# Reordering the build-time lists of stages, attention visits and PE transposes in a four-layer attention kernel

## The chip, the cores and the metric

One core of a Trainium2 chip; the experiments ran on three chips, each time with the kernel before in the same rounds. Time is device time of one execution in microseconds (us), the median of several executions. All executions told of here ran in the fast state; the mean clock granted to TensorE is 0.98 to 0.99 in every profile except one experiment, which is marked. Engines: PE is TensorE's matmul stream, PEld its weight loads, DVE is VectorE, ACT is ScalarE, POOL is GpSimd, SP is SyncE. "Attention run 1" and "attention run 2" are the two stretches with 1024 exponentials each (layers 1 and 3); the prediction calls them run 1 and run 2.

## The reference, cut to what matters

Four layers over x[2048, 1024], each with LayerNorm ahead and a residual after. Layers 0 and 2 (A) are linear attention with softmax feature maps, layers 1 and 3 (B) ordinary softmax attention; 32 heads of 32.

```python
def _A_ref(x, wqkv, w_phi, wo):          # linear attention
    # ... q, k, v: [1, 32, 2048, 32]
    pq = einsum("bhsd,hdf->bhsf", q, w_phi); pk = einsum("bhsd,hdf->bhsf", k, w_phi)
    phi_q = concat([softmax(pq), softmax(-pq)]); phi_k = concat([softmax(pk), softmax(-pk)])
    kv  = einsum("bhsf,bhsd->bhfd", phi_k, v);  z = phi_k.sum(s)
    o   = einsum("bhqf,bhfd->bhqd", phi_q, kv) / (einsum("bhqf,bhf->bhq", phi_q, z) + 1e-6)
    return o.reshape(B, S, D) @ wo
def _B_ref(x, wqkv, wo):                 # softmax attention
    p = softmax(einsum("bhqd,bhkd->bhqk", q, k) * 32 ** -0.5)
    return einsum("bhqk,bhkd->bhqd", p, v).reshape(B, S, D) @ wo

x = A_x
x = x + _A_ref(_layernorm(x), A_wqkv, A_w_phi, A_wo)
x = x + _B_ref(_layernorm(x), B_wqkv, B_wo)
x = x + _A_ref(_layernorm(x), A_wqkv, A_w_phi, A_wo)
x = x + _B_ref(_layernorm(x), B_wqkv, B_wo)
```

(Formulas shortened; the einsum that sums z over s is written out.)

## The kernel before

The file is a list scheduler. A clock model with generators runs while the program is built; `pick` takes the first ready task of a window, attention steps go ahead of tasks, and what comes out is one fixed order of instructions per engine. Three tables are its input:

- `STAGES`: the order of tasks. `AK` and `PQ`/`PS` are key and query work of an A layer by chunks of 512 rows, `DN` its denominators and numerators, `AO` its output tiles, `fold` a folding of weights; `('BP', layer, chunk, quarters)` is Q, K and V of a B layer, with eight head groups in four quarters; `('BO', layer, t0, t1)` its output tiles.
- `VIS1`, `VIS3`: attention visits of layers 1 and 3: first query tile, width in tiles, key chunks, whether it continues a partial sum, whether it is the last, and the head groups.
- `TR`: the chunks whose 128x128 transposes run on PE; all others go through a transposing DMA.

```python
def x_chain(l, t, key):                  # residual tile t behind layer l
    yield ("key", key)
    xb = yield from grab(t_x)
    yield dma(xb[:], xsrc(l, t), 256)
    # ... add, LayerNorm, store

def emit_step():                         # one attention step: score matmuls, then two exponentials
    u = units[st["ui"]]
    # ...
        for e in range(2):
            for j in range(2):
                # ...
                nc.tensor.matmul(ring_t[bufs[e]][:, j, i * n:(i + 1) * n], lhsT=K2[e][c]...,
                                 rhs=u.Q[r, e, 0:n], start=True, stop=True, ...)
    for e in range(2):
        clk.start(exp_chain(u, kks, e, bufs[e]), st["t"] + PE_LAT)

# in the main loop:
        if ready and len(ring.free) >= 2:
            emit_step()                  # attention first
            continue
        start_burst()
        if cur_u[0] is not None:
            emit_sum()                   # E.V and E.ones of earlier steps
            continue
        if cur[0] is None:
            cur[0] = pick()              # then a task of STAGES
        # ...
                if sum(x[1] for x in recent) < WARM * HAM:
                    set_mode("col")      # filler: nobody reads the result
                    for j in range(4):
                        nc.tensor.matmul(work[-1][32 * j:32 * (j + 1), :], lhsT=ones[:], rhs=idb, ...)

# in the Q projection's post, for the first two visits of layers 1 and 3 (three tokens in t_here):
                here = vi is not None and bool(t_here.free) and not t_here.wait
                if here:
                    # ... hand the Q tile to attention directly
                yield dma(qd[l, c, g][:], b2, 256)   # otherwise attention loads it back from DRAM
```

In a task's matmul group "full width" means one 128x128 matmul of 512 columns; while attention is active the group is issued as four narrow ones of 32 output rows each. A "score matmul" multiplies queries with keys; its result is what an exponential of attention reads.

The softmax here doesn't subtract the row's maximum and nothing guards it: scores larger than these inputs give would overflow.

## Time and profile before

| | before |
|---|---|
| median (3 executions) | 2384.27 us (2383.03 to 2387.67) |
| span of the profiled execution | 2380.4 us |
| front, until the first exponential of layer 1 | 289.4 us |
| attention run 1; of it ACT idle | 1003.0 us; 20.8 us |
| middle, between the two runs | 126.7 us |
| attention run 2; of it ACT idle | 953.1 us; 4.7 us |
| tail | 8.2 us |

In an attention run ACT is all but full; in front and middle PE and the waits of PE decide. The prediction shows the lines of the page.

### The profile page before, as it was taken

The numbers are of one execution on the slowest core, as the hardware profiler recorded it, in microseconds if no ns is written. First come the engines' busy times: TensorE is split into PE (matmuls) and PEld (weight loads), VectorE is DVE, ScalarE is ACT, GpSimd is POOL, SyncE is SP. The second block draws the span as 40 slices with busy tenths as digits, with TensorE's granted clock in tenths as the row PEclk, the third lists the DMA queues.
The fourth block names the chain that finished last, engine by engine and source line by source line (L and its number), as shares of the span: only waits on it lengthen the run. The fifth ranks groups of instructions, "written<-read, shape, count | busy, mean of one in ns | idle before, by whom it ended". The sixth has DMA issues, their size and how long they took to land.

```text
span 2380.4 us, 81956 instructions
## 1 busy us (share of the span) xinstructions
PE 2245.8 (94%) x35942; PEld 1009.7 (42%) x35985; DVE 1321.7 (56%) x2398; ACT 2121.0 (89%) x2501; POOL 400.5 (17%) x502
## 2 busy tenths in 40 slices
PE   6898999999999999998999899999999999999998
PEld 3544544334434333434555453433333333333555
DVE  6885554454545468696567855554533274363223
ACT  5543499999999999999998459999999999999998
POOL 3311101110211112122212210020200031120111
PEclk9999999899999999999999999999999999999999
DMA  6453364364454345354234655554465432230001
GB/s 249 145 157 108 132 193 171 112 199 130 147 141 145 108 133 155 115 142 80 91 101 130 173 135 166 192 140 137 123 198 174 135 125 81 64 110 33 19 22 31
DMA packets 216343, 306.05 MB, mean 129 GB/s; under 512 B 98736, under 2 KB 112560, under 8 KB 213296
## 3 DMA queue, kind: packets, MB, share of 16 engines
q1 hardware_dynamic: 191792, 200.14, 28.9%
q0 software_dynamic: 24192, 100.67, 12.6%
q8 instruction: 281, 4.60, 0.8%
q14 instruction: 78, 0.64, 0.1%
HBM read 195.36 MB, written 86.51 MB: 118 GB/s over the span
## 4 chain that ended last, share of the span: by engine, by line
PE 70%; ACT 16%; issue 7%; DVE 6%; DMA 1%; POOL 0%; SPq 0%; ACTq 0%; DVEq 0%; POOLq 0%
PE work L460 25%; PE work L1524 15%; ACT E L1449 14%; PE ring L1469 14%; PE work L463 7%; PE work L1642 3%; PE ring L463 3%; DVE blk L446 2%; ACT blk L772 1%; DVE sm L814 1%; PE work L1038 1%; DMA xnT<-blk 1%; DMA slab<-in_A_wqkv_dram 0%; DVE kvacc L446 0%; PE work L848 0%
## 5 line engine op out<-in xcount | busy, mean ns | idle before, releaser
L1449 ACT ACTIVATE E<-ring 128x1024 bf16<-128x1024 f32 x2048 | 1901.7, 1211 | 26.6 <-PE ring L1469 23.2
L1524 PE MATMUL work<-E,V 128*32 128x512 bf16 (+2 forms) x5888 | 551.1, 319 | 9.6 <-issue 3.7
L1524 PE MATMUL work<-E,ones 128*32 128x512 bf16 (+2 forms) x5888 | 551.0, 319 | 4.0 <-issue 4.0
L1469 PE MATMUL ring<-Q,K2b 32*128 32x512 bf16 (+2 forms) x2896 | 394.0, 315 | 49.4 <-ACT E L1449 38.1
L446 DVE TENSOR_TENSOR blk<-blk,work 128x512 f32<-128x512 f32 (+1 forms) x301 | 203.7, 680 | 375.5 <-PE work L1524 321.9
L1469 PE MATMUL ring<-Q,K2a 32*128 32x512 bf16 (+2 forms) x2896 | 407.8, 318 | 1.6 <-DMA Q<-qd 0.6
L1524 PEld LDWEIGHTS <-V 128*32 128x32 bf16 x5888 | 243.9, 97 | 158.0 <-issue 70.2
L446 POOL TENSOR_TENSOR blk<-blk,blk 64x512 bf16<-64x512 f32 (+2 forms) x180 | 175.1, 973 | 777.3 <-DVE blk L1314 689.4
L1278 DVE COPY blk<-work 128x512 f32<-128x512 f32 (+2 forms) x184 | 97.1, 528 | 346.4 <-PE work L1524 341.4
L1469 PEld LDWEIGHTS <-K2a 32*128 32x128 bf16 x2944 | 119.3, 91 | 385.1 <-issue 372.9
L1524 PEld LDWEIGHTS <-ones 128*32 128x32 bf16 x5888 | 239.5, 97 | 51.8 <-issue 5.9
L1314 DVE RECIPROCAL blk<-blk 128x128 f32<-128x128 f32 x254 | 229.4, 930 | 2.6
L1642 PE MATMUL work<-ident,ones 128*32 128x512 bf16 x3156 | 222.0, 382 | 2.8 <-DVE blk L446 0.9
L1469 PEld LDWEIGHTS <-K2b 32*128 32x128 bf16 x2944 | 163.3, 91 | 135.5 <-issue 128.7
L460 PE MATMUL work<-slab,blk 128*32 128x512 bf16 x2752 | 179.9, 381 | 0.5 <-DVE blk L1278 0.2
L460 PE MATMUL work<-slab,xnT 128*32 128x512 bf16 (+1 forms) x2560 | 156.5, 367 | 0.9 <-DVE kvacc L446 0.3
L460 PE MATMUL work<-xnT,slab 128*32 128x512 bf16 x2120 | 140.5, 384 | 4.2 <-DMA xnT<-blk 2.5
L463 PEld LDWEIGHTS <-xnT 128*128 128x128 bf16 x818 | 79.1, 99 | 89.9 <-issue 17.2
L460 PEld LDWEIGHTS <-blk 128*32 128x32 bf16 x3404 | 78.4, 96 | 90.5 <-issue 32.9
L463 PE MATMUL work<-slab,xnT 128*128 128x512 bf16 (+1 forms) x485 | 106.7, 373 | 5.5 <-DMA slab<-in_A_wqkv_dram 3.0
L1642 PEld LDWEIGHTS <-ones 128*32 128x32 bf16 x3156 | 71.2, 95 | 89.8 <-issue 40.7
L460 PEld LDWEIGHTS <-slab 128*32 128x32 bf16 x3016 | 70.8, 96 | 86.1 <-issue 35.8
(184 smaller groups left out, 2321.8 us busy)
## 6 DMA issues: line engine op xcount, KB each, us to landing
pd<-blk SPq DMA_DIRECT2D x154, 256.0 KB, 2.5
blk<-pd SPq DMA_DIRECT2D x154, 256.0 KB, 3.4
Q<-qd SPq DMA_DIRECT2D x121, 256.0 KB, 2.8
slab<-in_B_wqkv_dram POOLq DMA_DIRECT2D x30, 1024.0 KB, 6.6
qd<-blk SPq DMA_DIRECT2D x64, 256.0 KB, 2.8
x<-blk SPq DMA_DIRECT2D x48, 256.0 KB, 2.7
blk<-x SPq DMA_DIRECT2D x48, 256.0 KB, 3.8
blk<-in_A_x_dram SPq DMA_DIRECT2D x32, 256.0 KB, 3.9
```

Of the source, the lines that this page charges most:

```text
L446: return ("op", e, cost, lambda x: eng(x).tensor_tensor(out=o, in0=a, in1=b, op=op))
L460: nc.tensor.matmul(o[js], lhsT=l[:, js], rhs=r, start=st, stop=sp, tile_position=(0, 32 * j), skip_group_check=True)
L463: nc.tensor.matmul(o, lhsT=l, rhs=r, start=st, stop=sp, skip_group_check=True)
L772: yield ("op", "S", c_act(C), lambda x, s=s: nc.scalar.activation(out=e[:, s * C:(s + 1) * C], in_=src, func=ACT.Exp, scale=1.0 - 2.0 * s))
L814: yield ("op", "V", c_sb(1024), lambda x: nc.vector.reduce_sum(out=sm[:, 0:32], in_=e3, axis=AX.X))
L1038: nc.tensor.matmul(bank[:, o:o + P], lhsT=e[:, s * C + t * P:s * C + (t + 1) * P], rhs=kvm[:, (2 * gp + gi) * 2 + s, :], start=True, stop= ...
L1278: yield ("op", "V", c_ps(n), lambda e: nc.vector.tensor_copy(out=a, in_=bank[:, 0:n]))
L1314: yield ("op", "V", 0.06 + 0.0063 * P, lambda e, x=x: nc.vector.reciprocal(out=r[:, x:x + P], in_=r[:, x:x + P]))
L1449: yield ("op", "S", c_act(2 * n), lambda x: nc.scalar.activation(out=E[:, :, 0:n], in_=ring_t[buf][:, :, 0:n], func=ACT.Exp, scale=INV_SQR ...
L1469: nc.tensor.matmul(ring_t[bufs[e]][:, j, i * n:(i + 1) * n], lhsT=K2[e][c][u.g // 4][r, u.g % 4, m, :], rhs=u.Q[r, e, 0:n], start=True, st ...
L1524: nc.tensor.matmul(u.acc[r0 + 32 * j:r0 + 32 * j + 32, 0:n], lhsT=lh, rhs=E[:, j, i * n:(i + 1) * n], start=u.first, stop=end, tile_positi ...
L1642: nc.tensor.matmul(work[-1][32 * j:32 * (j + 1), :], lhsT=ones[:], rhs=idb, start=True, stop=True, tile_position=(0, 32 * j), skip_group_c ...
```

## The change

Its intent, in its own words: output tiles wait for all residual tiles of the preceding stage; a slab (1 MB of weights) that a ready task lacks is loaded at once; stages and visits come in another order. The tables are long; here the code parts whole and of the tables what the argument uses.

```diff
 def x_chain(l, t, key):
     yield ("key", key)
+    if l % 2:
+        for i in range(NT):
+            yield ("key", ("xo", l - 1, i))
     xb = yield from grab(t_x)
...
+def slab_rank(s):            # slab_next, plus PEN where the task still needs something
...
+def slab_force():            # load the slab of a ready task into a free slot
...
-        want = sorted((slab_next(s), s) for s in slab_use)
+        want = sorted((slab_rank(s), s) for s in slab_use)
...
+        if left and slab_force():          # only where the scheduler would report "stuck"
+            continue
         if left:
             ...
             raise RuntimeError(f"stuck at ...
+PEN = 0
...
 VIS1 = (      # 28 visits, now 36, the first four:
-    (0, 4, (0,), False, False, (4, 5)), (0, 4, (0,), False, False, (0, 1, 3)), (0, 4, (0,), False, False, (2,)),
-    (0, 4, (0,), False, False, (6, 7)), ...
+    (0, 4, (0,), False, False, (4, 5)), (0, 4, (0,), False, False, (0, 1, 3)),
+    (0, 4, (0,), False, False, (6, 7)), (0, 4, (0,), False, False, (2,)), ...
 VIS3 = (      # the first visits:
-    (0, 4, (0,), False, False, (4, 5)), (0, 4, (0,), False, False, (0, 1, 2, 3)),
-    (0, 4, (0,), False, False, (6, 7)), (0, 4, (1,), True, False, (0, 1, 2, 3)), ...
+    (0, 4, (0,), False, False, (0, 1, 2, 3, 4, 5, 6, 7)), (0, 4, (1,), True, False, (0, 1, 2, 3)), ...
 STAGES = (    # all reordered; the start, and the start of layer 3:
-    ('AK', 0, 0, (0,), (0,)), ('AK', 0, 1, (0,), (0,)), ('fold', ('pk', 0)), ('fold', ('pk', 1)), ...
-    ('DN', 2, 1), ('BP', 3, 0, (1,)), ('BP', 3, 0, (0,)), ('AO', 2, 2), ('BP', 3, 0, (2, 3)), ('AO', 2, 1), ...
+    ('AK', 0, 0, (0,), (0,)), ('AK', 0, 0, (0,), (1,)), ('AK', 0, 1, (1,), (0,)), ('fold', ('pk', 0)), ...
+    ('BP', 3, 0, (1,)), ('DN', 2, 1), ('BP', 3, 0, (0,)), ('BP', 3, 0, (2,)), ('AO', 2, 1), ('BP', 3, 0, (3,)), ...
-TR = {(0, 'D', 0), (0, 'D', 2), (0, 'D', 3), (0, 'K', 0), (0, 'K', 1), (0, 'O', 0), (0, 'O', 1), (0, 'O', 2), (1, 'B', 0), (2, 'D', 0), (2, 'D', 3)}
+TR = {(0, 'D', 0), (0, 'D', 1), (0, 'D', 3), (0, 'K', 0), (0, 'K', 1), (0, 'O', 0), (0, 'O', 2), (0, 'RQ', 1), (0, 'RQ', 3), (2, 'D', 0), (2, 'D', 3), (2, 'R', 0), (2, 'RQ', 0), (2, 'RQ', 1), (2, 'RQ', 3)}
```

(Cuts are marked by "..."; the keys with 'RQ' and 'R' are looked up nowhere.)

## The prediction

> **What bounds the kernel now.** The kernel is written by a small list scheduler that runs when the program is built: lists of stages and of attention visits go in, a fixed order of instructions per engine comes out. So I read first which engine sets the pace where, then what the lists change. First the head of the page.
>
> ```profile
> span 2380.4 us, 81956 instructions
> PE 2245.8 (94%) x35942; PEld 1009.7 (42%) x35985; DVE 1321.7 (56%) x2398; ACT 2121.0 (89%) x2501; POOL 400.5 (17%) x502
> ...
> L1449 ACT ACTIVATE E<-ring 128x1024 bf16<-128x1024 f32 x2048 | 1901.7, 1211 | 26.6 <-PE ring L1469 23.2
> ```
>
> PE looks like the bound at 94%, but 222.0 us of that is line L1642, filler matmuls whose result nobody reads; the scheduler puts them in to keep PE busy. The 2048 exponentials of attention on ACT cover 1901.7 us, in two runs of 1024 (layers 1 and 3). I found where each run begins and ends in the timeline of ACT (289.40 to 1292.35 and 1419.10 to 2372.20) and cut the span there. First all engines, then the exponentials alone (us of the stretch, then ACT busy).
>
> ```profile
> 0.00:289.40 289.40, 249.87 (x1817) 141.66 (x1849) 199.84 (x387) 131.50 (x239) 72.36 (x106) 0.98 0.48 160
> 289.40:1292.35 1002.95, 960.88 (x16687) 418.33 (x16689) 591.14 (x1022) 982.12 (x1105) 169.61 (x199) 0.98 0.45 132
> 1292.35:1419.10 126.75, 117.27 (x867) 63.65 (x876) 90.55 (x197) 58.99 (x120) 27.68 (x41) 0.97 0.63 173
> 1419.10:2372.20 953.10, 913.75 (x16560) 384.44 (x16557) 437.22 (x788) 948.36 (x1040) 130.89 (x156) 0.99 0.36 110
> 2372.20:2380.40 8.20, 4.05 (x31) 1.60 (x31) 2.90 (x5) 0.00 (x0) 0.00 (x0) 1.00 0.08 32
> ...
> 289.40:1292.35 1002.95, 960.09 (x1024) 0.98 0.45 132
> 1419.10:2372.20 953.10, 941.44 (x1024) 0.99 0.36 110
> ```
>
> Busy columns are PE, PEld, DVE, ACT, POOL. In the two attention runs ACT is busy 982.12 of 1002.95 and 948.36 of 953.10 us: it idles 20.8 and 4.7 us. In the first 289 us and the middle 127 us no exponential runs; PE is the busiest (250 and 117 us). The waits of ACT in the two runs name what little it lacks, and the chain of waits says what ends the middle: PE at full array width, unbroken.
>
> ```profile
> ACT E L1449 <- PE ring L1469: 19.9, 14, 4.8
> ...
> ACT E L1449 <- PE ring L1469: 3.3, 5, 1.0
> ...
> 1404.32 10.74 PE work L463 x49
> 1415.11 3.62 PE work L463 x16
> ```
>
> So the time is: front 289.4 (PE and its waits) + run 1 1003.0 (ACT) + middle 126.75 (PE) + run 2 953.1 (ACT) + tail 8.2. Only front, middle and 25 us of ACT idle can give.
>
> **What the Trainium skill says.** "ScalarE: Activation LUTs", section What ACT_TABLE_LOAD costs: an ACTIVATE with immediate scale takes 186 ns + 0.833 ns per element and neighbours overlap by about 93 ns, so an estimate from that page for 1024 elements is 946 ns a piece. The trace agrees: 35 exponentials in a row took 32.48 us, 928 ns each. They stand at their floor; no order makes them shorter. "TensorE: Matmul & The Clock Gate", section "Wait — 56ns, not 53.3ns?": 215.7 ns start to start for 512 columns when warm. The trace: 49 in 10.74 us, 219 ns each. "Perfetto Trace Analysis", section Identifying the Most-Contended Engine, warns that matmul busy share is no measure of headroom; here run 2 is 96% PE-busy and still ACT-bound. "Advanced Engine Details and Errata", section X-Bar Transpose (TRN2), says transposing DMAs are as fast as regular ones; here the transposes land in 3.5 us (median) and the 256 KB Q loads in 2.8 us, so nearly.
>
> **The change part by part.** I compared the built programs engine by engine, without their line numbers.
>
> 1. The wait of an output tile for all 16 residual tiles of the stage before. Taken alone on the new lists it changes nothing: with and without it the instructions and semaphore waits of all five engines are the same. The reason is in the data flow: an output tile of attention needs all 2048 keys, hence all 16 tiles of the stage before anyway. Cost 0.
> 2. Loading a missing slab at once: this branch runs only when the scheduler is stuck. Switched off, the program is the same. The slab ranking adds a penalty that is set to 0. Cost 0. The old code with the new lists gives the new program exactly, and the new code with the old lists the old one.
> 3. So everything is in the three lists: stages, visits, and the set of transposes on PE. I split both PE programs at the first and last score matmul of each layer and weigh each kind by the trace: 219 ns for 512 full-width columns, 58 ns for each of the four narrow ones, 54 ns per score matmul, 58 to 63 ns for the small ones.
>
> Front: 245.8 us of PE work before, 246.0 after. 64 fewer PE transposes (64 x 0.062 = 4.0 us), 5 output matmuls fewer (1.1), against 32 V matmuls of 256 columns (3.5) and 8 Q matmuls (1.75) more; on ACT 4 copies of 1.01 us fewer. The transposes now go through the DMA; while they are under way PE has the denominators and numerators of the next chunk, which had to be done before too. PE idled 289.4 - 249.9 = 39.5 us here, 20.3 of it in the first 60 us, where loads, LayerNorm and the folding of weights rule. The order of folding changes, its amount doesn't. I expect -1.5, give or take 6.
>
> Run 1: still 1024 exponentials and 80 other ACT halves (one per exp of the linear layer): the same list on ACT. PE work falls by about 5 us, but PE isn't the bound. Of 20.8 us of idle, waits of 2.5, 3.4, 3.5 and 4.8 us make most; they are accidents of one order, and some return elsewhere. A gap that the old list had at the very start (four full-width matmuls stood after the first score step) is gone. I take -3, give or take 7.
>
> Middle: here the lists do something I can count. PE work between the last score matmul of layer 1 and the first of layer 3 falls from 120.8 to 105.2 us. The first visit of layer 3 started with head group 4, behind all eight K and seven Q projections; it now starts with group 0 behind four K and three Q projections (8 x 219 ns = 1.75 us each; together with four V projections 512 wide that became six of half the width, this is 95 matmuls of 219 ns fewer and 48 of 110 ns more, 15.6 us). Middle: 126.75 - 15.6 = 111.
>
> Run 2: the same work comes back in its first 64 exponentials, 51.6 before and 67.1 after, 37 of the matmuls at full width. That width is used only where attention stalls, so the new order says itself that it stalls. From the program: step 1; Q and K projection; steps 2 and 3; Q; step 4; then V, K, Q and two output tasks, 0.94 + 4 x 1.75 = 7.9 us; step 5. A step is two exponentials, 1.86 us of ACT, and 0.65 us of PE. Laid end to end, step 5 is ready at about 15.7 us, while eight exponentials need 7.4: ACT idles some 8.3 us. After that, PE work per 64 exponentials is about 50 us against 59.4 of ACT, as before. Run 2: 953.1 + 8.3 = 961.4. The visits also get wider (1152 instead of 1536 narrow score matmuls), but run 2 is held by ACT, so that buys nothing.
>
> Tail: same 64 + 16 matmuls, 8.2.
>
> Sum of differences: -1.5 - 3 - 15.6 + 8.3 + 0 = -11.8 us, or -0.5%. 2384.3 - 11.8 = 2372.5; I say 2373.
>
> **The rivals.** (a) The earlier start is worth nothing: steps 1 to 4 run early and ACT then waits for exactly the projections that were skipped. For: 15.5 us of the work returns. Against: eight exponentials are through by then. It would leave 2380. (b) The lists repair the front and run 1: if half of the 39.5 us PE idle and most of the 20.8 us ACT idle went, about 20 + 15 more, 2340. For: a new list is likely picked because some measure liked it. Against: amounts and rough order of folding and linear attention are the same, and dependencies through DVE (busy 20.0 of 20 us from 60 to 80 us) stay. (c) New stalls: more slab loads on the POOL queue (514 rows against 507), 12 more partial results out and 12 in, 8 more DMA transposes, shared buffers. For: one late load cost 4 to 8 us in places before (a transposed tile near 683 us took 7.9). Against: the DMA share in run 1 is 0.45. Two or three such stalls give 2390.
>
> **Range and chances.** Errors of about 6 in the front, 7 in run 1, 4 in middle and run 2 together, 4 for run-to-run spread (2383.03 to 2387.67) give about 11 in the square sum, and a margin for what I have not seen: 2354 to 2388 should hold it 8 times in 10. Faster by 2% would need 47.7 us, nearly all of the front's idle time and of ACT's: 2 in 100. Slower by 2% needs a handful of new stalls at once: 2 in 100. Within 2%: 96 in 100.
>
> **What would show it.** In the new profile the same five stretches: front near 288, run 1 near 1000, middle near 111, run 2 near 961 with one wait of ACT of about 6 us for the score matmuls after its eighth exponential. Exponentials 928 ns apart as before. It is wrong if the middle stays above 120 (then it wasn't PE work), if run 2 stays at 953 or goes over 970, or if the front or run 1 moves by more than 10 us: then order alone made or removed waits that counting work doesn't see.

## More of the kernel before

One more line is needed later: the page's row for the instruction queue (packets, MB, share of the DMA engines).

```profile
q8 instruction: 281, 4.60, 0.8%
```

281 packets of 16 KB: PE and PEld together executed 35942 + 35985 = 71,927 instructions, 256 for each packet (255.5 to 256.4 in all profiles of this case). So q8 brings PE's program, and at 33 instructions per us in attention run 1 (16687 + 16689 in 1003 us) a packet lasts about 7.7 us.

## The result, and the profile after

After: 2366.76 us, median of 4 executions (2364.45 to 2373.36). Before, in the same rounds: 2383.65 us (2382.35 to 2387.67). The ratio is 0.9931, with a 95% interval of 0.9907 to 0.9955. Ratios here and below are the mean time of one kernel's fast runs over that of the other's of the same rounds, so not quite the ratio of the medians. The result is 0.7% faster, inside 2%.

The head of the page after, to be set against the one in the prediction:

```profile
span 2366.3 us, 81613 instructions
PE 2240.7 (95%) x35742; PEld 1014.3 (43%) x35782; DVE 1329.3 (56%) x2419; ACT 2108.6 (89%) x2483; POOL 410.4 (17%) x509
...
L1494 ACT ACTIVATE E<-ring 128x1024 bf16<-128x1024 f32 x2048 | 1899.6, 1218 | 20.1 <-PE ring L1514 18.1
```

The exponentials still take 1899.6 / 2048 = 928 ns each. Nothing on this page explains the 14 us of span; the five stretches do. The kernel after, cut as before (stretch, its length, then PE, PEld, DVE, ACT, POOL busy with their counts, TensorE clock, DMA share, GB/s):

```profile
0.00:285.96 285.96, 248.26 (x1789) 141.51 (x1820) 199.55 (x389) 124.28 (x232) 77.69 (x114) 0.98 0.55 167
285.96:1278.15 992.19, 954.95 (x16672) 418.47 (x16673) 587.73 (x1021) 981.91 (x1104) 174.79 (x205) 0.99 0.44 134
1278.15:1389.89 111.74, 101.83 (x823) 59.19 (x825) 88.79 (x190) 48.62 (x98) 27.76 (x41) 0.97 0.59 168
1389.89:2356.50 966.61, 930.20 (x16443) 393.02 (x16442) 450.37 (x816) 953.72 (x1050) 130.12 (x149) 0.99 0.39 118
2356.50:2366.30 9.80, 5.43 (x31) 2.11 (x31) 2.90 (x5) 0.09 (x1) 0.00 (x0) 0.83 0.07 27
```

The middle is 15 us shorter, as counted. But attention run 2 is 13.5 us longer and eats that up: ACT has ten more instructions there (1050 against 1040), 5.4 us more work (953.7 against 948.4), and idles 12.9 us instead of 4.7. What is left of the gain comes from the front (3.4 us) and, unexpectedly, from attention run 1 (10.8 us), where ACT does the same work (981.9 against 982.1) and idles 10.3 us instead of 20.8. The waits of ACT for score matmuls, first in attention run 1, then in run 2 (total, times, longest):

```profile
ACT E L1494 <- PE ring L1514: 9.3, 10, 4.0
...
ACT E L1494 <- PE ring L1514: 8.8, 10, 2.1
```

Before they were 19.9 us in 14 waits and 3.3 us in 5.

### The profile page after: what moved, and what is told of

It reads as the page before. It is cut to its first block, busy times and chain, and to the rows that moved or that the text cites. A ratio compares the mean times of both kernels' runs of the same rounds, so it can differ in the third digit from the quotient of the medians.

```text
span 2366.3 us, 81613 instructions
## 1 busy us (share of the span) xinstructions
PE 2240.7 (95%) x35742; PEld 1014.3 (43%) x35782; DVE 1329.3 (56%) x2419; ACT 2108.6 (89%) x2483; POOL 410.4 (17%) x509
## 3 DMA queue, kind: packets, MB, share of 16 engines
q0 software_dynamic: 24080, 99.62, 12.8%
## 4 chain that ended last, share of the span: by engine, by line
PE 39%; ACT 10%; issue 5%; DVE 2%; DMA 0%; SPq 0%; ACTq 0%; POOL 0%; DVEq 0%; POOLq 0%
PE work L464 14%; ACT E L1494 10%; PE work L1569 9%; PE ring L1514 8%; PE work L467 3%; PE work L1687 2%; PE ring L467 1%; DVE blk L450 1%; PE work L1083 0%; PE work L893 0%; DVE blk L1359 0%; DVE sm L859 0%; ACT blk L817 0%; PE ring L1083 0%; DVE blk L1323 0%
## 5 line engine op out<-in xcount | busy, mean ns | idle before, releaser
L1494 ACT ACTIVATE E<-ring 128x1024 bf16<-128x1024 f32 x2048 | 1899.6, 1218 | 20.1 <-PE ring L1514 18.1
L1514 PE MATMUL ring<-Q,K2b 32*128 32x512 bf16 (+2 forms) x2776 | 389.0, 319 | 44.0 <-ACT E L1494 31.9
L450 DVE TENSOR_TENSOR blk<-blk,work 128x512 f32<-128x512 f32 (+1 forms) x316 | 214.1, 681 | 374.4 <-PE work L1569 304.4
L1514 PE MATMUL ring<-Q,K2a 32*128 32x512 bf16 (+2 forms) x2776 | 398.5, 322 | 0.9 <-ACT E L1494 0.6
L464 PE MATMUL work<-xnT,slab 128*32 128x512 bf16 x2324 | 154.0, 385 | 3.5 <-DMA xnT<-blk 3.0
L464 PE MATMUL work<-slab,xnT 128*32 128x512 bf16 (+1 forms) x2520 | 142.4, 350 | 5.0 <-issue 1.5
L467 PEld LDWEIGHTS <-xnT 128*128 128x128 bf16 x884 | 85.8, 99 | 89.5 <-issue 19.4
```

The costliest lines, as they stand in the source:

```text
L450: return ("op", e, cost, lambda x: eng(x).tensor_tensor(out=o, in0=a, in1=b, op=op))
L464: nc.tensor.matmul(o[js], lhsT=l[:, js], rhs=r, start=st, stop=sp, tile_position=(0, 32 * j), skip_group_check=True)
L467: nc.tensor.matmul(o, lhsT=l, rhs=r, start=st, stop=sp, skip_group_check=True)
L1494: yield ("op", "S", c_act(2 * n), lambda x: nc.scalar.activation(out=E[:, :, 0:n], in_=ring_t[buf][:, :, 0:n], func=ACT.Exp, scale=INV_SQR ...
```

## The experiments

Three questions. Which part of the change carries what: the code, the first half of the lists, the second half (theory: the lists of the first half carry all, and the second half is a wash; rival: the middle's 15 us are the gain)? Why does attention run 1 idle less (theory: the order; rival: accidents of the execution, such as where the fetching of instructions and the DMA transfers happen to fall)? And why does run 2 give back what the middle gains (theory: the same PE work has merely moved; rival: one slow route, Q through DRAM, which could be mended)?

Before any run, built programs were compared engine by engine: the new code with the old lists has the same instructions and waits as before, the old code with the new lists the same as after. The first run asks whether the chip agrees. All kernels below gave correct results.

### e1_code_only: new code, old lists

```diff
-VIS1, VIS3, STAGES, TR of after
+VIS1, VIS3, STAGES, TR of before
```

> The new code (the wait for all residual tiles, the forced slab load) with the old lists: instruction for instruction the kernel before. Theory (code parts cost nothing): ratio 1.000 within 0.15%. It is also a second execution of the old program: if ACT's waits in run 1 (3.4 us after exponential 285, 3.5 after 416, 4.8 after 881, 20.5 us in all) come from the order, they return at the same places within 1 us; the rival (they are accidents of one execution) expects the ones that the chain calls issue, 285 and 881, to be gone or elsewhere and run 1 to be up to 8 us shorter in this profile.

Measured: 2381.97 us, ratio 0.9990 (0.9974 to 1.0006): the code alone is worth nothing that can be seen. But its profile is a lesson in itself: the same program on the same input showed attention run 1 at 995.2 us (ACT idle 13.6), against 1003.0 (20.8) in the profile of before. One profile of each of two kernels cannot settle a difference of 8 us in one stretch; the medians and several profiles have to.

### e2_new_first and e3_new_second: each half of the lists alone

```diff
 # e2, on after:
-STAGES from ('BO', 1, 7, 9) on, and VIS3: new
+STAGES from there on, and VIS3: old  (with ('BO', 1, 5, 7) for ('BO', 1, 5, 6), so that each tile comes once)
 # e3, on before:
-STAGES from ('BP', 1, 3, (3,)) on, and VIS3: old
+STAGES from there on, and VIS3: new  (without ('BO', 1, 6, 7), which had come already)
```

> New lists up to the end of layer 1, old ones from there. Theory (the two halves act apart, and run 1's gain belongs to its new order): front 286 and run 1 992 as in the changed kernel, middle 127 and run 2 953 as before, so about 2370 us, -14. Rival (run 1's gain in the profile was luck of one execution, as my prediction's -3 would have it): run 1 near 1000 and a time near 2379.

> Old lists up to the end of layer 1, new ones from there. Theory (PE work moved from the middle into run 2 comes back as idle ACT): middle 112, run 2 966, time -1 to -3 us, near 2382. Rival (what leaves the middle is won, since PE has slack in run 2): middle 112, run 2 953, time near 2369.

Measured: e2 2369.25 us, ratio 0.9941 (0.9927 to 0.9956); e3 2380.05 us, ratio 0.9989 (0.9975 to 1.0003). So the first half carries the gain and the second none that can be seen. The windows from the start of attention run 1 on, of e2 and then of e3, with columns as above:

```profile
287.10:1275.57 988.47, 952.71 (x16673) 418.54 (x16676) 588.45 (x1020) 981.07 (x1105) 176.26 (x205) 0.99 0.44 135
1275.57:1401.43 125.86, 116.45 (x867) 63.15 (x872) 90.62 (x197) 58.83 (x119) 27.77 (x41) 0.97 0.62 174
1401.43:2353.30 951.87, 911.73 (x16556) 384.63 (x16552) 437.05 (x788) 947.85 (x1040) 130.90 (x156) 0.99 0.36 110
```

```profile
292.50:1294.80 1002.30, 957.50 (x16684) 417.82 (x16685) 591.51 (x1023) 982.05 (x1104) 169.46 (x199) 0.99 0.45 132
1294.80:1406.37 111.57, 101.69 (x823) 59.16 (x828) 88.67 (x190) 48.59 (x98) 27.66 (x41) 0.97 0.58 168
1406.37:2373.32 966.95, 930.45 (x16443) 391.74 (x16442) 450.16 (x816) 953.94 (x1050) 129.87 (x149) 0.99 0.39 118
```

Read the second and third line of each: middle plus run 2 is 125.9 + 951.9 = 1077.7 us with the old second half, 111.6 + 967.0 = 1078.5 with the new. The middle's gain is real, and in these two profiles it is worth nothing.

### e4_swap_only and e8_g0first: starting attention of layer 3 sooner or later

```diff
 # e4, on before: VIS3's first two visits exchanged
-    (0, 4, (0,), False, False, (4, 5)), (0, 4, (0,), False, False, (0, 1, 2, 3)),
+    (0, 4, (0,), False, False, (0, 1, 2, 3)), (0, 4, (0,), False, False, (4, 5)),
 # e8, on after: the first projections of layer 3 exchanged
-    ('BP', 3, 0, (1,)), ('DN', 2, 1), ('BP', 3, 0, (0,)),
+    ('BP', 3, 0, (0,)), ('DN', 2, 1), ('BP', 3, 0, (1,)),
```

> The kernel before with nothing but the first two visits of layer 3 exchanged, so that head group 0 comes first. Theory: this one exchange is what empties the middle: PE work there 104.8 us as in the changed kernel, middle near 111, run 2 near 965, time within 4 us of before. Rival (the middle needs the new stage order too): middle stays near 127 and run 2 near 953.

> The changed kernel with the K and Q of head groups 0 and 1 projected before those of 2 and 3 in layer 3. PE work in the middle falls by count from 105.2 to 95.4 us, the first 64 exponentials carry 76.9 instead of 67.1. Theory: groups 0 and 1 then hold places, the middle is near 101 and run 2 longer by what PE lacks, 2 to 6 us: 4 to 8 us under the changed kernel, near 2360. Rival (the work comes back in full): middle 101, run 2 977, time as the changed kernel.

Measured: e4 2386.82 us, ratio 1.0009 (0.9995 to 1.0023); middle 110.6, run 2 973.0 with ACT idle 18.5. e8 2371.42 us, ratio 0.9957 (0.9939 to 0.9975); middle 101.6, run 2 979.4 with ACT idle 21.2. The swap of two visits is enough for the whole effect on the middle, and e8 pushes it 10 us further. In either case run 2 takes it back: e8's run 2 is 12.8 us longer than after's. So e8's rival came true, not its theory.

### e7_here4_l3: Q of the second head group not through DRAM

In after, the three tokens for a direct hand-over of Q are taken by head groups 2, 3 and 0, and group 1, which attention needs next, goes out to DRAM and back. This gives a fourth token for layer 3.

```diff
+                if l == 3 and vi is not None and not more_here:
+                    more_here.append(1)
+                    t_here.give(0)
                 here = vi is not None and bool(t_here.free) and not t_here.wait
```

> The changed kernel with one more place, in layer 3 alone, for a Q tile that is handed to attention without the way through memory. In the changed kernel groups 2, 3 and 0 take the three places, and group 1, which the third unit needs, is stored and loaded again (each 2.8 us). Theory (this way, not the amount of PE work, makes ACT wait after eight exponentials): step 5 follows at once, ACT's idle time in run 2 falls from 13 to under 7 us, run 2 from 966.7 to about 960, time 5 to 7 us under the changed kernel, near 2361. Rival (my prediction: 7.9 us of projections stand in the way whatever their order): run 2 stays at 966.

Measured: 2367.99 us, ratio 0.9951 (0.9934 to 0.9968), no better than after; run 2 is 965.0 us (ACT idle 11.5) against 966.6 (12.9). First the timeline of ACT in after where run 2 begins (start, length, instructions, and in brackets the idle time ahead and what ended it), then the one of e7:

```profile
1398.20 1.96 ACT L1494 ACTIVATE E<-ring 128x1024 bf16<-128x1024 f32 x2
1401.57 0.37 ACT L443 CAST K2a<-work 128x256 bf16<-128x256 f32 x1 [1.41 <-PE work L467]
1401.95 0.74 ACT L443 CAST K2b<-work 64x256 bf16<-64x256 f32 x2
1403.34 0.59 ACT L443 CAST blk<-ring 128x512 bf16<-128x512 f32 x1 [0.64 <-issue]
1405.99 51.46 ACT L1494 ACTIVATE E<-ring 128x1024 bf16<-128x1024 f32 x56 [2.07 <-PE ring L1514]
```

```profile
1395.88 38.77 ACT L1498 ACTIVATE E<-ring 128x1024 bf16<-128x1024 f32 x42
...
1438.17 0.37 ACT L443 CAST V<-work 128x256 bf16<-128x256 f32 x1 [1.33 <-PE work L467]
1439.42 1.94 ACT L1498 ACTIVATE E<-ring 128x1024 bf16<-128x1024 f32 x2 [0.88 <-PE ring L1518]
```

In after there are 5.8 us between the eighth exponential and the ninth (1400.16 to 1405.99), 4.1 of it idle. With the fourth token that gap is gone: 42 exponentials follow one another. But the waits only move to behind the 48th or so, and the sum falls by 1.4 us. The projections that were put off still have to be done before attention can go on.

### e5_shift64 and e10_after_shift64: the same program, its fetching shifted

In before, ACT loses about 5 us near the 881st exponential of attention run 1. First the timeline of PE there, two lines of a row of equal matmuls; then the chain of waits:

```profile
1123.47 0.28 PE L1524 MATMUL work<-E,V 128*32 128x256 bf16 x2
1127.76 0.29 PE L1524 MATMUL work<-E,ones 128*32 128x256 bf16 x2 [4.02 <-issue]
```

```profile
1122.76 0.98 PE work L1524 x30
1123.75 4.02 issue
1127.76 0.94 PE work L1524 x18
```

PE stops for 4 us and waits for nothing that the profile shows. At that time the instruction queue was late: packets started at 1112.2 and 1125.4, 13 us apart (the median in attention run 1 is 7.6, and half of the distances lie between 5.9 and 9.1), and PE went on 1.2 us after the second was in (it took 1.15 us). The DMA engines were crowded; the issues between 1110 and 1120 us in before, then between 1100 and 1110 in after, where the same pile lies (output, input, queue, count, KB each, median us to landing):

```profile
slab<-wf_pq POOLq DMA_DIRECT2D x2, 1024.0 KB, 11.0
x<-blk SPq DMA_DIRECT2D x1, 256.0 KB, 13.7
...
xnT<-blk SPq DMA_TRANSPOSE x2, 10.9
```

```profile
slab<-wf_pq POOLq DMA_DIRECT2D x2, 1024.0 KB, 9.6
x<-blk SPq DMA_DIRECT2D x1, 256.0 KB, 13.1
...
xnT<-blk SPq DMA_TRANSPOSE x2, 10.3
```

Over the whole execution such a slab lands in 6.3 us, a store of x in 2.7, a transpose in 3.5 (medians). In after, the pile was as heavy, but three packets started at 1098.4, 1106.5 and 1114.3, and PE stopped for only 1.47 us, until 1.4 us after the third was in. That suggests a rival for all of attention run 1: not the order but the phase of fetching. So 64 tiny matmuls with their weight loads ahead of everything, half a packet, in before (e5) and in after (e10):

```diff
+    for _ in range(64):
+        nc.tensor.matmul(work[-1][0:32, 0:32], lhsT=ones[:], rhs=ones[:], start=True, stop=True,
+                         tile_position=(0, 0), skip_group_check=True)
```

> The kernel before with 64 dummy matmuls (128 PE instructions with their weight loads) at the start, where PE waits for its first data: every later PE instruction stands 128 places further back, nothing else changes. In all four kernels with the old first half PE stops for 4 to 7 us within a row of score-times-V matmuls near exponential 881 though it waits for nothing, and goes on about 1.2 us after an instruction packet landed; two 1 MB slab loads, two DMA transposes and a store are under way then. Theory (PE ran out of instructions because its fetch came due inside that pile of transfers): the fetch comes due at another time, the stop near 881 falls under 1.5 us or moves, run 1 changes by some 3 to 8 us. Rival (the pile itself holds PE, through a wait that the profile does not show): the stop near 881 stays at 4 to 7 us. The front costs at most 2 us more.

> The changed kernel with the same 64 dummy matmuls at the start as the shifted old one. If the 10 us that run 1 gains are the luck of where PE's instruction fetches fall, the shift gives stops of 3 to 7 us back and run 1 goes to about 1000, the time up by 5 to 10 us. If they belong to the new order (fewer waits of ACT whatever the fetches do), run 1 stays at 988 to 994 and the time within 4 us of the control.

Measured: e5 2378.99 us, ratio 0.9997 (0.9981 to 1.0014), attention run 1 at 1002.0 us with 19.6 idle. The stop near exponential 881 is gone, but a transpose that landed late took its place elsewhere (the chain of waits of e5):

```profile
679.15 11.80 DMA xnT<-blk
```

e10: 2369.95 us, ratio 0.9955 (0.9939 to 0.9970), attention run 1 at 991.8 with 10.3 idle (a wait of 4.3 us near exponential 881 included). Shifting the fetch moves neither kernel's time beyond the noise, so the gain is not a matter of the phase of fetching.

Whether PE lacked instructions at these stops can be counted in the kept traces. In none of the 14 profiles has PE executed more than 405 instructions (matmuls and weight loads) beyond 256 for each packet landed. Thirteen stops of PE in attention run 1, in ten of the profiles, come just when this excess is 400 to 405, and each ends 1.2 to 1.5 us after the next packet is in. The stop in e5 for which the chain names a transpose came at an excess of 181. So PE stops near exponential 881 because its next instructions are late. That the pile makes them late fits and was not isolated: in e5 the pile was also lighter (slabs 7.5 us, transposes 6.1).

### e6_gap_k2: one more chunk's transposes off the DMA

```diff
-TR = {..., (2, 'D', 0), (2, 'D', 3)}
+TR = {..., (2, 'D', 0), (2, 'D', 3), (2, 'K', 2)}
```

> The kernel before with the four transposes of layer 2's chunk 2 on PE (32 small matmuls, 2 us of PE with slack) in place of four DMA transposes, which are part of the pile near exponential 881. Theory (fetch held up by the pile): the slab loads and the store there land in under 10 us instead of 13.8, and PE's stop is under 1.5 us; run 1 near 997. Rival (the two slab loads alone make the pile): landings stay near 13 us and the stop stays at 4 us or more.

Measured: 2397.11 us, ratio 1.0074 (1.0055 to 1.0093). In attention run 1 it does what it should: no stop near 881, 995.2 us with 12.4 idle (e1's profile of the old program had 995.2 too, so this saving may be chance). But the middle grows to 139.4 us and run 2 to 959.8. Two waits of PE in the middle are the largest there, each on a transposing DMA of another chunk:

```profile
PE ring L463 <- DMA xnT<-blk: 4.4, 1, 4.4
PE work L463 <- DMA xnT<-blk: 3.5, 1, 3.5
```

One entry of a table shifted later decisions of the scheduler; what was saved in one stretch was lost twice over in others.

### e9_after_again: after without the forced load

```diff
-        if left and slab_force():
+        if False and slab_force():
```

> The changed kernel with the forced slab load switched off: the same instructions as the changed kernel. It is the control for the next run on the same chip and a further execution of the new program. Theory: ratio 0.993 to 0.995; run 1 988 to 993 with no stop of PE over 2 us beside the one near exponential 413.

The built program is the same as after's. Measured: 2366.78 us, ratio 0.9943 (0.9927 to 0.9958); attention run 1 at 994.6 us with 13.0 idle. Here a wait of 4.59 us before an exponential near the 881st is back, in the new order, and the chain names a transpose that took 16.14 us. That misses the expectation (988 to 993, no other stop over 2 us). So the idle time near 881 is partly chance in both orders, and it has more than one cause.

### e11_tr_only: the new set of PE transposes on the old stages

```diff
-TR of before
+TR of after                       # VIS1, VIS3, STAGES stay old
```

> The new code with the new set of PE transposes, but the old stages and visits: four chunks' transposes before layer 1 partly go to the DMA as in the changed kernel. Theory (the first half's gain comes from the new order of stages and visits): front 289 to 293 and run 1 995 to 1003, time within 4 us of before. Rival (it is the transposes taken off PE and ACT): front 286 and run 1 near 992, time 10 us or more under before.

Measured: 2433.87 us, ratio 1.0222 (1.0204 to 1.0240), the only kernel clearly over 2% slower. Attention run 1 is 1038.7 us with ACT idle 52.9. The waits of PE in that run, then POOL's timeline at the second stop:

```profile
PE work L574 <- DMA slab<-in_B_wqkv_dram: 26.5, 2, 13.5
```

```profile
855.20 2.59 POOL L557 TENSOR_TENSOR blk<-blk,blk 64x512 bf16<-64x512 f32 x2 [31.04 <-DVE blk L1466]
857.73 0.93 POOL L539 DMA_DIRECT2D slab<-in_B_wqkv_dram  x1
```

POOL issues the weight loads, in order with its own tensor work. An operation that waited for DVE held the issue of a slab back, and PE stood still twice for some 13 us. The middle grew too, to 141.2 us; only the front, 290.8 us, came out as the theory had it, and neither theory nor rival had the time. The lists are one coupled set: what is good with the new stages is the worst of all with the old.

### e12_no_filler: after without the unread matmuls

```diff
-WARM = 0.7
+WARM = 0.0
```

> The changed kernel without its 3144 filler matmuls, about 170 us of PE streaming by count. My reading of the profile (the two runs are bound by ACT, whatever PE's busy share says): PE's share falls from 95% to some 85 to 90% and the time stays within 6 us of the control. Rival (PE is the bound, as its 95% says): 20 us or more faster. Second rival (the filler keeps PE's clock up): granted clock below 0.95 and 10 us or more slower.

Measured: 2423.45 us, ratio 1.0180 (1.0162 to 1.0199). Attention run 2 (one window, columns as above) and the row of the granted clock in 40 slices:

```profile
PEclk9999999999999799999999999899999676776868
...
1399.12:2411.32 1012.20, 889.82 (x13895) 353.68 (x13894) 452.77 (x815) 963.61 (x1051) 132.99 (x153) 0.83 0.37 117
```

My reading that the filler is worthless was wrong. Without it PE has 2548 matmuls fewer in run 2, is busy 88% of it instead of 96%, and the granted clock falls from 0.99 to 0.83; the score matmuls come late and ACT idles 48.6 us instead of 12.9. The second rival came true. The Trainium skill ("TensorE: Matmul & The Clock Gate", section What's actually happening) says that the clock is gated by how busy PE has been recently; this run agrees, with 0.99 at 96% and 0.83 at 88%.

## Why the prediction was right or wrong

The predicted 2373 stands against 2366.76, the -0.5% against -0.7%. The stretches of all profiles (us; in brackets ACT idle):

| profile | front | run 1 | middle | run 2 | tail |
|---|---|---|---|---|---|
| before | 289.4 | 1003.0 (20.8) | 126.7 | 953.0 (4.7) | 8.2 |
| e1, same program | 290.8 | 995.2 (13.6) | 127.6 | 952.4 (4.2) | 8.3 |
| e5, shifted | 289.7 | 1002.0 (19.6) | 125.4 | 953.4 (5.1) | 9.7 |
| e3, new second half | 292.5 | 1002.3 (20.2) | 111.6 | 967.0 (13.0) | 8.4 |
| e4, visits swapped | 293.5 | 1003.0 (21.0) | 110.6 | 973.0 (18.5) | 8.4 |
| e2, new first half | 287.1 | 988.5 (7.4) | 125.9 | 951.9 (4.0) | 8.8 |
| e7, fourth token | 286.4 | 989.4 (7.9) | 111.8 | 965.0 (11.5) | 8.4 |
| e8, group 0 first | 289.4 | 991.0 (9.5) | 101.6 | 979.4 (21.2) | 9.7 |
| e10, after shifted | 290.6 | 991.8 (10.3) | 110.6 | 966.1 (12.5) | 8.3 |
| e9, same program as after | 289.5 | 994.6 (13.0) | 111.0 | 965.7 (12.2) | 8.3 |
| after | 286.0 | 992.2 (10.3) | 111.7 | 966.6 (12.9) | 9.8 |

**The code parts, cost 0: right.** Shown by the identical programs and by e1.

**Front, predicted -1.5: right in kind.** -3.4 in the pair; the five rows with the old first half average 291.2 us, the six with the new 288.2, so -3.0, with 4 to 5 us of scatter inside either group (the clock of the front differs from profile to profile, and so do the chips), so the size is rough. PE's busy time in the front fell by 2.0 us on average (251.7 to 249.8), where the prediction counted no less work, and its idle time only by 1.0 (39.4 to 38.4). Which work or wait went was not followed up.

**Attention run 1, predicted -3: a term of the sum that was mis-sized, threefold.** The same groups average 1001.1 (idle 19.0) and 991.3 (idle 9.7): -9.9 us, 9.3 of it ACT idle, and e2, e5 and e10 show that it comes with the new first half and not with the phase of the fetch. The pair's 10.8 us even trips the prediction's own sign of being wrong (run 1 moves by more than 10 us: order removed waits that counting work doesn't see). By place, old average less new: 3.8 us in the first 100 us, 2.2 between 100 and 420 us of the run, 3.2 around the 881st exponential (800 to 860 us), 0.2 in the rest. The first is order: every old profile shows it and no new one. Its main part, at 53 us, is not the gap at the very start that the prediction names (0.4 us, also gone), but the 2.5 us that it counts among the accidents of one order. The chain of waits of before, and the timelines of ACT of before and then of after at that place:

```profile
343.41 0.81 PE ring L463 x3
344.22 0.33 PE ring L1469 x4
```

```profile
329.03 13.13 ACT L1449 ACTIVATE E<-ring 128x1024 bf16<-128x1024 f32 x14
344.64 1.94 ACT L1449 ACTIVATE E<-ring 128x1024 bf16<-128x1024 f32 x2 [2.48 <-PE ring L1469]
```

```profile
333.64 11.24 ACT L1494 ACTIVATE E<-ring 128x1024 bf16<-128x1024 f32 x12
345.28 7.44 ACT L1494 ACTIVATE E<-ring 128x1024 bf16<-128x1024 f32 x8 [0.40 <-PE ring L1514]
```

Task matmuls, the last three of them at full width (L463), stood ahead of the score matmuls (L1469) and the exponentials waited 2.5 us; after, 0.4. With the other waits of the first 100 us it is 4.2 in all five old profiles and 0.4 in all six new ones.

By cause, most of the rest is late instructions. Behind stops of PE at an excess of 400 to 405, ACT idles 8.2, 6.0, 1.7, 9.0 and 7.8 us in the old profiles (before, e1, e5, e3, e4) and 0.9, 0, 1.1, 1.2, 4.3 and 0 in the new ones (after, e2, e7, e8, e10, e9): 6.5 and 1.2 on average, 5.3 of the 9.3 us. Near the 881st and without the shift, PE stops after 29,329 instructions in the old order (for 4.0 to 7.0 us) and after 29,331 in the new (for 1.5 to 1.8), so the phase is the same and the packet is less late. Why it is less late is not shown, and part is chance: around the 881st, old profiles show 0 to 8.8 us of idle time, new ones 0 to 4.9. In e5 the stops nearly went and the median did not move; its late transpose cost 7.4 us of idle time. Where the step failed was in saying "some return elsewhere" of waits without saying how many: the new order lost half of them and made few new.

**Middle, predicted -15.6 by counting matmuls: right.** -15.0 in the pair, and -15.1 from the average of the four profiles with the old second half as it was (before, e1, e5, e2: 126.4) to that of the five with the new one as it is (after, e3, e7, e9, e10: 111.3).

**Attention run 2, predicted +8.3: the second mis-sized term.** It was +13.6. The predicted term was ACT idle, and that came out at +8.2 (4.7 to 12.9), with the first wait where it was predicted, after the eighth exponential, and 4.1 us of idle there; the rest of the idle time lies in smaller waits behind it. Left out was ACT's own work: casts and the exponential halves of layer 2 that used to lie in the middle, where ACT was free, now stand among the exponentials: 953.7 less 948.4, +5.4 us. Counting only PE's work was the mistake: "no exponential runs" in the middle is true of attention's alone, and 64 halves of layer 2's ran there in before (four of them, and six casts, are what moved). So middle and run 2 together go from an average of 1079.5 (before, e1, e5) to 1077.2 (after, e7, e9, e10), a gain of 2.3 us where 7.3 was predicted (about 1.6 if e2 and e3, which have crossed halves, are counted in). The first rival, that the earlier start is worth nothing, was nearly right, and e7 and e8 show why: it is the amount of PE and ACT work before attention can flow, not its place or its route.

**Wider visits buy nothing: right** (run 2 has no fewer idle microseconds). **Tail 0:** 8.2 to 9.8 us in all profiles, in no relation to the lists.

**The second rival**, that the lists repair front and run 1, was half right: half of ACT's idle time in run 1 went, but of the 39.5 us of PE's in the front only 1.8 in the pair. **The third**, new stalls, did not come in after; e11 shows that it was a real danger, with the same TR set.

The sum: -3.0 - 9.9 - 2.3 = -15 from the averages of profiles; -16.9 from the medians of the first measurement, and about -12.4 for the same program on another chip (e9 against 2379.21). Predicted -11.8: two errors of opposite sign, 7 in run 1 and 5 in run 2, nearly cancelled, so that the total came out so close is partly luck.

No version beats after: e2, e7 and e9 all lie at 0.994 to 0.995 with intervals that overlap.

## What to carry to other kernels

Where one engine is full for a long stretch, work moved out of the gap before it into its first microseconds is not saved (e3, e4 and e8 here); add up the work of all engines on both sides of the border, the bound one's own small casts included. A stretch that differs by 8 us in single profiles of the same program needs several profiles or a half-and-half experiment before a cause is named. Tables that feed a list scheduler are one coupled set: one of them alone cost 2.2% here, and a single entry 0.7%.

## What the Trainium skill lacked or had wrong

- "Runtime: NRT & Kernel Launch", section Instruction fetch mechanics, gives blocks of 16 KiB or 256 instructions, with which the 281 packets for 71,927 PE instructions agree, and calls the cost of a boundary "mostly hidden". It says nothing of a fetch behind other transfers: before shows a stop of PE of 4.02 us, e1, e3 and e4 stops of 4.97, 7.03 and 4.74 us at the same place, with nothing to wait for; in before the packets started 13 us apart (median 7.6), while slabs took 8.0 and 13.9 us. The traces show that PE stops when it has executed 400 to 405 instructions beyond 256 for each landed packet, and goes on 1.2 to 1.5 us after the next one. What makes the packet late was not shown by itself.
- "Advanced Engine Details and Errata", section X-Bar Transpose (TRN2), says transposes are as fast as regular DMAs. That nearly holds at the median (3.5 us, against 2.8 for a 256 KB load of Q), and in a pile of two 1 MB loads both suffer (transposes 10.3 to 16.1 us, a 256 KB store 13.1 to 13.7). No page gives a time to landing under such load.
- "TensorE: Matmul & The Clock Gate" says what the clock follows, but not what unread matmuls are worth in a kernel bound by another engine: here attention run 2 went from 966.6 to 1012.2 us without them, with the clock from 0.99 to 0.83 and PE still busy 88% of the time.
